# Attention and an ELU feed-forward on one core: where the first two head pairs get their decay sums, and products that nobody reads at the start

## The chip, the cores and the metric

The kernel runs on one core of a Trainium2 chip. Its time is the device time of one execution in microseconds. A core has a matrix engine (TensorE, PE in the profile), a vector engine (VectorE, DVE), a scalar engine (ScalarE, ACT), a general engine (GpSimd, POOL), a queue that issues transfers (SyncE, SP), and 16 DMA engines that carry them.

## The reference, cut to what matters

```python
# q, k, v: 8 batches x 8 heads x 576 rows x 64;  s: 8 x 8 x 576
scores = matmul(q, k.T) / 8
cum    = cumsum(maximum(s, 0))                       # the decay sums, one row per head
bias   = -(cum[..., :, None] - cum[..., None, :])
scores = where(causal, -1e9, scores + minimum(bias, 0))
attn   = softmax(scores)                             # with 1e-9 added to the sum
x      = (attn @ v) as 4608 rows x 512
h      = x @ w_in                                    # 512 x 2048
g      = where(h > 0, h, exp(minimum(h, 0)) - 1)
out    = g @ w_out                                   # 2048 x 512
```

In a causal row the part of the bias that belongs to the query is the same for all keys, and the softmax takes it away. What must be added to the scores is one number per key and head: the head's decay sum.

## The kernel before, in words

Heads are worked in pairs. The first rows (0 to 319, `LOW`) of batches 0 to 2 are done by the class `Low`, twelve units of one pair each; pair 0 and pair 1 of batch 0 are the program's first work. A pair has five score products: one for the first 64 rows of both heads (128 columns) and one per head for two blocks of 128 rows (192 and 320 columns), 1,152 columns together. They are in float32, which TensorE does with two records per product in the trace. VectorE masks each block, scales it and takes the row's minimum (`softmax_block`, line 872), ScalarE takes the exponential with its sum (line 877), VectorE inverts the sums (lines 882 and 883), and any engine scales the block (`normalize`, lines 890 to 894). TensorE then turns the blocks with an identity matrix (lines 680 and 694, tiles `trl`), ScalarE or VectorE copies the turned blocks out of PSUM (lines 381 and 382, tiles `tl`), and TensorE multiplies them with the values (line 675, tile `avl`). After that comes the other attention work and, from 92 us on, the feed-forward (lines 1165 and 1203), which fills most of the time.

The decay sums of a pair ride along in the score product: the tile of keys `kl` has 64 rows of keys, one more row (row 64) with the two heads' sums, and zeros below; the tile of queries `ql` has ones there. Pair 0's sums are worked out alone by `first()` on one partition (lines 430 to 434) and written straight into the row of `kl_first`. All 64 heads' sums are worked out afterwards on 64 partitions in `aux` (lines 445 to 447). Pair 1 gets its row by a transfer from `aux`, every later pair by a transfer from a copy in DRAM, `aux_dram`. Two buffers hold the keys of these units (tag `st`), so pair 2's keys are loaded when pair 0's last score product is done.

Nobody wrote the order by hand. `Plan.issue` keeps a clock for each engine, with a fixed cost for each operation, and always takes the operation that could start first; among those that start together the lower `prio` wins. The order so found is fixed for each engine, and each engine works its list strictly in order. SyncE, too, issues its transfers in that order, and an issue that waits for a buffer holds up all behind it. The weights of the feed-forward come in 512 KB pieces, each with two instructions on VectorE and one on ScalarE to turn it into float32 (lines 531 to 537) and two to split it. Their loads wait for `urgent`, the transfer of pair 1's row.

Blocks of scores may take any of seven PSUM banks (tags `a`, `h`, `o0`, `o1`, `o2`); a turned block may take only the two of tag `a`.

Of the kernel before, what the change touches and what calls it, by code (L numbers as in the profile page):

```python
# [17 lines left out]
P = 128  # L18
# [24 lines left out]
PRIO_LOW = 10  # L43
SP_COST = 430.0

N_FREE = 0


class Buf:
# [18 lines left out]


class Op:  # L70
    __slots__ = ("ways", "after", "before", "behind", "bufs", "new", "prio", "ready", "left")


class Plan:
# [33 lines left out]
    def op(self, prio, ways, reads=(), writes=(), late=()):  # L108

        o = Op()  # L110
        o.ways, o.prio = ways, (prio, len(self.ops))
# [36 lines left out]
        return o  # L148
# [8 lines left out]
    def issue(self):  # L157
# [17 lines left out]
        last = {}  # L175
        n_done = 0
        while pending:
            best = None
            held = slots.get(self.signal, ())
            busy = free["PE"] > DYN_T or held and held[-1].users and not held[-1].others  # L180
            for o in pending:
# [16 lines left out]
                else:  # L198
# [95 lines left out]
def pool_1(n):  # L294
    return 120 + 1.04 * n
# [7 lines left out]
def kernel(  # L303
# [108 lines left out]
        return k, [("Pool-M", pool_1(2 * LOW), lambda: pool.memset(k.v[HB:], 0.0))]  # L412


    k_first, cleared = low_keys("first")

    def decay_sums():

        own = slice(HB, HB + 1)

        def row(m):
            return aux.v.rearrange("p m t -> p (m t)")[own, 2 * m * LOW : 2 * (m + 1) * LOW]

# [13 lines left out]
        def sp():  # L437
            return aux.v[:NB, 0]

        def lo():  # L440
            return aux.v[:NB, 1]

        op(-10, [("DVE-SB", 2700.0, first)], [], [(aux, "row"), (k_first, "sums")])
        for cost, step in (
            (460.0, lambda: dve.tensor_scalar(sp(), sp(), 0.0, None, ALU.max)),
            (1350.0, lambda: dve.tensor_tensor_scan(lo(), sp(), sp(), 0.0, ALU.add, ALU.max)),
            (590.0, lambda: dve.tensor_scalar(
                sp(), lo(), lo()[:, S // 2 : S // 2 + 1], 8.0, ALU.subtract, ALU.mult)),
        ):
            op(-9, [("DVE-SB", cost, step)], [], [(aux, 0), (aux, 1)])  # L450
        load(15, lambda: aux_dram.v[:, 0], sp, [(aux, 0)], [(aux_dram, 0)], NB * S * 4)

    def decay_parts():

        sp, lo, hi = (lambda m=m: aux.v[:NB, m] for m in range(3))
        op(20, [("DVE-SB", 850.0, lambda: dve.tensor_scalar(hi().bitcast(F32R), sp(), 1.0, None, ALU.mult))],
           [(aux, 0)], [(aux, 2)])
        op(20, [("DVE-SB", 750.0, lambda: dve.tensor_tensor(lo().bitcast(F32R), sp(), hi(), ALU.subtract))],
           [(aux, 0), (aux, 2)], [(aux, 1)])
        for m in (2, 1):  # L460
            load(20, lambda m=m: aux_dram.v[:, m], lambda m=m: aux.v[:NB, m], [(aux, m)],
                 [(aux_dram, m)], NB * S * 4)

    def ones():
# [130 lines left out]
    def prepare_low(u):  # L595

        b, j, prio = u.b, u.j, u.prio
        u.vs = vs[u.turn]
        u.k, clear = (k_first, None) if (b, j) == (0, 0) else low_keys(u.tag)
# [5 lines left out]
        op(prio if b or j else -10, [("Pool-M", pool_1(2 * LOW), lambda: pool.memset(u.q.v[HB:], 1.0))],  # L605
           [], [(u.q, "ones")])
        if (b, j) > (0, 0):
            op(prio, clear, [], [(u.k, "sums")])

            src = aux if (b, j) == (0, 1) else aux_dram  # L610
            o = load(prio, lambda: u.k.v[at],
                     lambda: src.v[h0 : h0 + 2, 0, :LOW],
                     [(src, 0)], [(u.k, "sums")], 2 * LOW * 4)
        if (b, j) == (0, 1):
            urgent.append(o)
        n = 1 + 2 * (1 + CUT)

# [7 lines left out]
    def scoring_low(u):  # L625
# [2 lines left out]
        u.first = plan.buf(sb, [P, P], F32, f"pl_{u.tag}", tag=("khs", "vs0")[u.turn])  # L628
        u.pp = {}
        tiles = [(u.first, P)]  # L630

        def pair():
            softmax_block(
                prio, f"{u.tag}_0", True, u.first, P, masks,
                lambda o, w: masks.v.rearrange("p h t -> p (h t)"), [u.k, u.q],
                lambda o, w: ((u.q.v[:, :P], u.k.v[:, :, :HB]),),
                (sm, 0, False, 0, 1.0), view=lambda v: v.rearrange("p (h t) -> p h t", h=2),
            )

        def block(i, h):  # L640
# [8 lines left out]
            if h or u.turn:  # L649
# [2 lines left out]
            softmax_block(  # L652
                prio, f"{u.tag}_{n}", True, pt, pw[i], maskw,
                lambda o, w: maskw.v[:, max(WM - pw[i] + o, 0) :][:, :w], [u.k, u.q],
                lambda o, w: ((u.q.v[:, at], u.k.v[:, h, o : o + w]),),
                (sm, n, n == 2 * CUT, 1 + 2 * CUT, 1.0),
            )
            if n == 2 * CUT:
                for col, (pt, w) in enumerate(tiles):
# [198 lines left out]
    def softmax_block(prio, tag, native, pt, w, mask, mv, reads, operands, inv, view=lambda v: v):  # L858

        n = 1 if w <= 512 else 2  # L860
        mn = plan.buf(sb, [P, 2], F32, f"mn_{tag}", tag="mn", bufs=3)
# [1 line left out]
        for i in range(n):  # L863
            sc = score_bank(f"sc_{tag}_{i}")

            def scores(i=i, sc=sc):
                pairs = operands(i * cw, cw)
                for n, (l, r) in enumerate(pairs):
                    pe_.matmul(view(sc.v[:, :cw]), l, r, start=n == 0, stop=n == len(pairs) - 1)  # L869

            op(prio, [("PE", pe4(cw) if native else 2 * pe(cw), scores)], reads, [sc])
            op(prio, [("DVE", 84 + dve_p(cw), lambda i=i, sc=sc: dve.tensor_tensor_reduce(  # L872
                pt.v[:, i * cw : (i + 1) * cw], sc.v[:, :cw], mv(i * cw, cw), scale,
                BIG if i == 0 else mn.v[:, 0:1], ALU.add, ALU.min, mn.v[:, i : i + 1]))],
               [sc, mask], [(pt, "data"), mn])
# [212 lines left out]
    def attention():  # L1088
# [20 lines left out]
        for u, prepared, scored, weighed in todo:  # L1109
# [5 lines left out]
                behind = []  # L1115
            was = type(u)
            now = scored(u)
            if u is todo[1][0]:
                decay_parts()
            for n in range(max(len(now), len(behind))):  # L1120
                for step in (now[n : n + 1] + behind[n : n + 1]):
                    step()
            behind = weighed(u)
        for step in behind:
            step()
# [120 lines left out]
                t += n  # L1246
        return following

    decay_sums()
    zeros()  # L1250
    mask_tiles()
    for i in range(NQ):
# [93 lines left out]
```

## Time and profile before

| | us |
|---|---|
| median of three runs | 1131.26 |
| lowest and highest | 1130.28, 1135.73 |
| profiled execution | 1133.43 |
| its span in the trace | 1131.7 |
| PE busy | 1096.9 (97%) |
| DVE busy | 843.3 (75%) |
| ACT busy | 628.1 (55%) |
| POOL busy | 451.1 (40%) |

The span is what the trace covers; the execution's own time is 1.7 us longer. The busy time of an engine is the sum of its instructions; what PE lacks to the span, 34.8 us, is the time in which it stood still. A granted clock of 1.00 is 2.4 GHz and 0.50 is 1.2 GHz; a product at 0.50 counts as busy all the same, so the busy share doesn't show the clock.

### The profile page before, as it was taken

Reading aid. Unit: us, or ns where it says so; the run is one execution under the profiler, and the core shown is the slowest. Engines: PE = TensorE matmul, PEld = TensorE weight load, DVE = VectorE, ACT = ScalarE, POOL = GpSimd, SP = SyncE. Lnnn points to the kernel's source line nnn. Section 1 sums busy time; section 2 is a strip of 40 time slices with the busy share of each in tenths; the row PEclk is TensorE's granted clock in tenths of the full one; section 3 lists DMA queues with packets and bytes.
Section 4 is the critical chain, followed back from the end, with each engine's and each line's share of the span. In section 5 each row is a group of like instructions: output and inputs, shape, how many; then the busy total and the mean of one; then the engine's idle time right before and its main releaser. Section 6 shows DMA issues by size and latency. Waiting matters only on the chain.

```text
span 1131.7 us, 19748 instructions
## 1 busy us (share of the span) xinstructions
PE 1096.9 (97%) x5992; PEld 951.6 (84%) x5992; DVE 843.3 (75%) x2133; ACT 628.1 (55%) x1525; POOL 451.1 (40%) x657
## 2 busy tenths in 40 slices
PE   6888999999999999999999999999999999999998
PEld 5677877888788888788888888888888888999997
DVE  6888999778887877687977787878888888432322
ACT  4786766456555655555555555655655556433433
POOL 6664475336444433344434434525544433100000
PEclk8899999999999999999999999999999999999999
DMA  6887688756756855765555666567787686210000
GB/s 173 225 213 201 172 189 193 157 113 152 161 125 128 186 130 121 180 127 133 149 133 118 175 140 136 122 143 172 160 200 155 138 189 151 56 56 1 28 1 28
DMA packets 341689, 156.52 MB, mean 138 GB/s; under 512 B 266424, under 2 KB 320464, under 8 KB 341584
## 3 DMA queue, kind: packets, MB, share of 16 engines
q1 hardware_dynamic: 341584, 155.27, 59.6%
q8 instruction: 48, 0.79, 0.3%
q14 instruction: 57, 0.47, 0.1%
HBM read 79.66 MB, written 19.32 MB: 87 GB/s over the span
## 4 chain that ended last, share of the span: by engine, by line
PE 63%; DVE 6%; DMA 2%; issue 1%; ACT 1%; POOL 1%; SPq 0%; POOLq 0%; DVEq 0%; ACTq 0%
PE o L1203 26%; PE h L1165 25%; PE av L1000 7%; PE sc L869 5%; DVE p L930 2%; DMA stq<-in_qT_dram 1%; DMA T<-p 1%; DVE p L872 1%; DVE h L1187 1%; DVE xl L374 1%; DVE qs L374 0%; DVE x_None L1084 0%; DVE gl L1190 0%; DVE vs L374 0%; DVE g L1182 0%
## 5 line engine op out<-in xcount | busy, mean ns | idle before, releaser
L1165 PE MATMUL h<-xh,wi 128*128 128x384 f32 x1536 | 445.5, 340 | 1.4 <-DVE gl L1190 1.3
L1203 PE MATMUL o<-wo,gh 128*128 128x512 f32 x1152 | 362.5, 396 | 0.1
L1165 PEld LDWEIGHTS h<-xh,wi 128*128 128x128 f32 x1536 | 283.0, 188 | 9.9 <-DVE gl L1190 3.0
L1165 PE MATMUL h<-xl,wi 128*128 128x384 f32 x768 | 258.8, 337 | 0.0
L1203 PEld LDWEIGHTS o<-wo,gh 128*128 128x128 f32 x1152 | 207.3, 188 | 27.4 <-DVE mn L872 0.5
L1203 PE MATMUL o<-wo,gl 128*128 128x512 f32 x576 | 227.8, 395 | 1.0 <-DVE gl L1190 0.8
L1187 DVE SCALAR_TENSOR_TENSOR h<-h,g 128x384 f32<-128x384 f32 x192 | 107.9, 562 | 122.2 <-ACT g L1178 120.6
L1173 ACT ACTIVATE g<-h 128x384 f32<-128x384 f32 x192 | 94.1, 490 | 177.5 <-PE h L1165 167.4
L877 ACT ACTIVATE p<-p,mn 128x192 f32<-128x192 f32 (+1 forms) x232 | 144.9, 625 | 75.1 <-DVE mn L872 72.0
L930 DVE SCALAR_TENSOR_TENSOR p<-p,sm,p 128x512 f16<-128x512 f32 (+3 forms) x239 | 170.7, 742 | 7.6 <-POOL p L922 4.5
L1165 PEld LDWEIGHTS h<-xl,wi 128*128 128x128 f32 x768 | 144.6, 188 | 6.7
L922 POOL TENSOR_SCALAR p<-p,sm 128x512 f16<-128x512 f32 (+3 forms) x125 | 86.9, 702 | 134.3 <-DVE sm L883 53.1
L381 ACT CAST gh<-h 128x384 fp32r<-128x384 f32 x175 | 83.5, 477 | 87.8 <-DVE h L1187 86.6
L1190 DVE TENSOR_TENSOR gl<-h,gh 128x384 fp32r<-128x384 f32 x192 | 106.0, 552 | 32.9 <-ACT gh L381 31.7
L1203 PEld LDWEIGHTS o<-wo,gl 128*128 128x128 f32 x576 | 108.2, 188 | 25.8 <-DVE gl L1190 2.3
L872 DVE CUSTOM_DVE_ANT_0 p<-sc,maskw 128x192 f32<-128x192 f32 (+1 forms) x232 | 109.8, 483 | 25.8 <-PE sc L869 21.4
L1000 PE MATMUL av<-T,vs 128*128 128x256 f16 (+5 forms) x896 | 119.2, 285 | 2.9 <-DMA T<-p 2.1
L1000 PEld LDWEIGHTS <-vs 128*128 128x128 bf16 x896 | 79.7, 98 | 49.8 <-issue 14.3
L375 POOL TENSOR_TENSOR vs<-vs 128x320 f32<-128x320 f32 x72 | 61.0, 848 | 124.6 <-DMA vs<-in_vb_dram 72.1
L869 PE MATMUL sc<-kh,qs 128*128 128x192 f32 (+2 forms) x272 | 87.5, 326 | 2.9 <-DVE mn L872 2.5
L869 PE MATMUL sc<-k,q 128*128 128x192 f32 (+2 forms) x272 | 83.9, 312 | 2.2 <-DMA q<-qs 1.3
L1178 ACT ACTIVATE g<-g 128x384 f32<-128x384 f32 x138 | 72.5, 525 | 4.2
(145 smaller groups left out, 1365.3 us busy)
## 6 DMA issues: line engine op xcount, KB each, us to landing
stk<-in_kT_dram SPq DMA_DIRECT2D x64, 288.0 KB
vs<-in_vb_dram SPq DMA_DIRECT2D x64, 160.0 KB
stq<-in_qT_dram SPq DMA_DIRECT2D x40, 256.0 KB
w_i<-in_w_in_dram SPq DMA_DIRECT2D x16, 512.0 KB
w_o<-in_w_out_dram SPq DMA_DIRECT2D x16, 512.0 KB
out_dram<-ost SPq DMA_DIRECT2D x32, 256.0 KB
x_dram<-x_None SPq DMA_DIRECT2D x20, 288.0 KB
q<-qs SPq DMA_DIRECT2D x40, 128.0 KB
```

Of the source, the lines that this page charges most:

```text
L381: ("ACT", act_c(n), lambda: act.copy(dst(), src())),
L869: pe_.matmul(view(sc.v[:, :cw]), l, r, start=n == 0, stop=n == len(pairs) - 1)
L872: op(prio, [("DVE", 84 + dve_p(cw), lambda i=i, sc=sc: dve.tensor_tensor_reduce(pt.v[:, i * cw : (i + 1) * cw], sc.v[:, :cw], mv(i * cw, c ...
L877: op(prio, [("ACT", 480 + w / 1.2, lambda: act.activation(pt.v[:, :w], pt.v[:, :w], AF.Exp, bias=mn.v[:, n - 1 : n], scale=-1.0, accum_out ...
L922: ("Pool", 160 + 1.04 * n, lambda part=part: pool.tensor_scalar(part(t16, 0), own(part), sm.v[:, r], 1.0, ALU.mult, ALU.mult)),
L930: ("DVE-SB", dve_2(n), lambda part=part: dve.scalar_tensor_tensor(part(t16, 1), own(part), sm.v[:, r], part(t16, 0), ALU.mult, ALU.subtract)),
L1000: op(prio, [("PE", cost, lambda m=m, operands=operands, rows=rows: pe_.matmul(av.v[:rows, dst], *operands(), start=first and m == 0, stop= ...
L1165: pe_.matmul(hp.v[:, :TC], w_in_f[f].v[:, part, c * P : (c + 1) * P], xx.v[:, c, :TC], start=(c == 0 and m == 0), stop=(c == NCB - 1 and m ...
L1173: op(side, [("ACT", act_c(TC), lambda: act.activation(g.v[:, :TC], hp.v[:, :TC], AF.Exp))], [hp], [g])
L1187: op(side, [("DVE", dve_p(TC), lambda: dve.scalar_tensor_tensor(hp.v[:, :TC], hp.v[:, :TC], 0.0, g.v[:, :TC], ALU.max, join[0]))], [g], [hp])
L1190: op(side, [("DVE", dve_p(TC), lambda: dve.tensor_tensor(gl.v[:, :TC], hp.v[:, :TC], gh.v[:, :TC].bitcast(F32), ALU.subtract))], [hp, gh], ...
L1203: pe_.matmul(acc[i].v, g.v[:, tb], w_out_f[f].v[:, part], start=(f == 0 and m == 0), stop=(f == NF - 1 and m == 2),)
```

## The change

Pairs 0 and 1 no longer have a row of sums in their keys. After each score product a second product is added into the same PSUM bank: its stationary operand is `pick`, a 128 x 128 tile with ones in one row (copied from the identity), its moving operand is the first 128 rows of `aux`, of which `pick` selects the head's. This is `picked_sums`, line 651. So `first()` goes, and with it pair 1's transfer. The sums on 64 partitions are worked out in two parts: the first 320 columns at once, the others later (`high()`), after the last masking of the second unit. `aux_dram` gets the first 320 columns alone.

The second part adds transposes of the identity into a PSUM tile that nothing reads, `scratch`. Up to 300 are offered to the planner with the lowest priority and a start that counts as later than it is by `GAP`; those left when the planner's own clock passes `FILL_T` are thrown away. In the order that results there are 31: the first, 28 in a row behind it, and two more. The loads of the first two blocks of weights no longer wait for `urgent` (`N_FREE`), and `urgent` is now pair 2's row.

```diff
-N_FREE = 0
+N_FREE = 2
+FILL_T, GAP = 22e3, 350.0
+N_FILL = 300
+N_PICK = 2
...
+            if free["PE"] > FILL_T:
+                for o in [o for o in pending if o.filler]:
+                    pending.remove(o)
...
-                    rank = (start, o.prio)
+                    rank = (start + GAP if o.filler else start, o.prio)
...
+    picks = [plan.buf(sb, [P, 2, P], F32, f"pick_{j}", tag="gh", bufs=2) for j in range(N_PICK)]
...
-        def first():
-            dve.tensor_scalar(row(0), row(0), 0.0, None, ALU.max)
-            for h in range(2):
-                sp, lo = (row(m)[:, h * LOW : (h + 1) * LOW] for m in range(2))
-                dve.tensor_tensor_scan(lo, sp, sp, 0.0, ALU.add, ALU.max)
-                dve.tensor_scalar(k_first.v[own, h], lo, lo[:, S // 2 : S // 2 + 1], 8.0,
-                                  ALU.subtract, ALU.mult)
...
+        def low():
+            dve.tensor_scalar(sp(first), sp(first), 0.0, None, ALU.max)
+            summed(first)
...
+        for j, t in enumerate(picks):
+            op(-10, [("Pool", 400.0, lambda j=j, t=t: pool.tensor_copy(
+                t.v, ident[:, 2 * j : 2 * j + 2].unsqueeze(2).to_broadcast([P, 2, P])))], [], [t])
...
+        def picked_sums(sc, parts):
+            def step():
+                for n, (h, to, keys) in enumerate(parts):
+                    pe_.matmul(sc.v[:, to], u.pick.v[:, h], aux.v[:, 0, keys],
+                               start=False, stop=n == len(parts) - 1)
...
+    def fillers():
+
+        scratch = plan.buf(ps, [P, DM], F32, "scratch", tag="o2")
+        op(-20, [("PE", 111.0, lambda: pe_.transpose(scratch.v[:, :P], ident, ident))], [], [scratch])
+        for n in range(N_FILL):
+            o = op(1e6 + n, [("PE", 160.0, lambda: pe_.transpose(scratch.v[:, :P], ident, ident))], [(scratch, None)], [])
+            o.filler = True
```

Since the planner deals out all operations by time, the order of all engines differs from there to the end. Three places matter here. The first is PE's first instructions (`sc_0_` and `sc_1_` are the score blocks of pairs 0 and 1). Before:

```order
L869 MATMUL sc_0_0_0_121<-kl_first,ql_0_85 128x128
L869 MATMUL sc_0_1_0_128<-kl_first,ql_0_85 128x192
L869 MATMUL sc_0_2_0_133<-kl_first,ql_0_85 128x192
L869 MATMUL sc_0_3_0_144<-kl_first,ql_0_85 128x320
L869 MATMUL sc_0_4_0_150<-kl_first,ql_0_85 128x320
L869 MATMUL sc_1_0_0_181<-kl_1_89,ql_1_99 128x128
```

And now:

```order
L1281 MATMUL scratch<-ident 128x128
L1283 MATMUL scratch<-ident 128x128 x28
L895 MATMUL sc_0_0_0_156<-kl_0_78,ql_0_85 128x128
L651 MATMUL sc_0_0_0_156<-aux,pick_76 128x64 x2
L895 MATMUL sc_0_1_0_165<-kl_0_78,ql_0_85 128x192
L651 MATMUL sc_0_1_0_165<-aux,pick_76 128x192
```

Twenty-nine transposes stand ahead of pair 0, and each score product has a second one behind it, for pairs 0 and 1. The second place is PE at the scores of pairs 2 and 3 (`trl_1_1` is a turned block of pair 1). Before, after pair 2's fourth block:

```order
L694 MATMUL trl_1_0_307<-ident,p_81 128x128
L694 MATMUL trl_1_0_307<-ident,p_112 128x128
L694 MATMUL trl_1_0_307<-ident,pl_0_1_110 128x128
L694 MATMUL trl_1_0_307<-ident,pl_0_1_135 128x128
L675 MATMUL avl_1_314<-tl_1_303,vs_92 128x128
L694 MATMUL trl_1_1_320<-ident,p_81 128x128
```

And now:

```order
L720 MATMUL trl_1_0_360<-ident,pl_0_1_183 128x128
L895 MATMUL sc_3_0_0_370<-kl_3_267,ql_3_277 128x128
L895 MATMUL sc_3_1_0_376<-kl_3_267,ql_3_277 128x192
L895 MATMUL sc_3_2_0_383<-kl_3_267,ql_3_277 128x192
L895 MATMUL sc_3_3_0_390<-kl_3_267,ql_3_277 128x320
L895 MATMUL sc_3_4_0_394<-kl_3_267,ql_3_277 128x320
L720 MATMUL trl_1_1_427<-ident,p_94 128x128
```

All of pair 3's scores have moved ahead of pair 1's second turned block, and pair 1's products with the values (`avl_1`) behind it. The third place is ACT, where the copy of pair 1's first turned block into `tl_1` stands. Before:

```order
L531 ACTIVATE w_o_201<-w_o_201 128x512
L381 COPY tl_1_303<-trl_1_290 128x128
L877 ACTIVATE pl_2_286,sml_2_305<-pl_2_286,mn_2_0_287 128x128
L877 ACTIVATE p_76,sml_2_305<-p_76,mn_2_1_296 128x192
L877 ACTIVATE pl_0_2_240,sml_2_305<-pl_0_2_240,mn_2_2_312 128x192
```

And now:

```order
L905 ACTIVATE pl_2_342,sml_2_352<-pl_2_342,mn_2_0_343 128x128
L905 ACTIVATE p_89,sml_2_352<-p_89,mn_2_1_350 128x192
L905 ACTIVATE pl_0_2_289,sml_2_352<-pl_0_2_289,mn_2_2_368 128x192
L905 ACTIVATE p_91,sml_2_352<-p_91,mn_2_3_373 128x320
L905 ACTIVATE pl_0_2_297,sml_2_352<-pl_0_2_297,mn_2_4_381 128x320
L905 ACTIVATE pl_3_387,sml_3_397<-pl_3_387,mn_3_0_388 128x128
L549 ACTIVATE w_i_328<-w_i_328 128x512
L922 ACTIVATE p_89<-p_89,sml_2_352 128x192
L922 ACTIVATE pl_0_2_297<-pl_0_2_297,sml_2_352 128x320
L401 COPY tl_1_422<-trl_1_354 128x128
```

The copy stood ahead of pair 2's exponentials and stands behind all five of them now, behind one of pair 3's, a piece of weights and two scalings of pair 2.

## Rows read from the trace of the kernel before

**Rows 1.** The profile's page: span, and busy time by engine.

```profile
span 1131.7 us, 19748 instructions
PE 1096.9 (97%) x5992; PEld 951.6 (84%) x5992; DVE 843.3 (75%) x2133; ACT 628.1 (55%) x1525; POOL 451.1 (40%) x657
```

**Rows 2.** Table by stretch: length, PE, PEld, DVE, ACT, POOL busy, PE's clock, DMA, GB/s.

```profile
0.00:6.47 6.47, 0.00 (x0) 0.03 (x1) 3.32 (x6) 1.28 (x1) 5.50 (x24) 1.00 0.44 112
6.47:10.42 3.95, 3.95 (x10) 2.85 (x10) 3.42 (x10) 1.05 (x5) 3.71 (x11) 1.00 0.76 137
10.42:14.19 3.77, 0.01 (x2) 0.03 (x1) 3.21 (x10) 2.19 (x7) 2.16 (x5) 0.90 0.43 114
14.19:20.30 6.11, 6.11 (x21) 5.23 (x22) 1.53 (x8) 2.30 (x8) 0.41 (x2) 0.50 0.95 270
20.30:30.54 10.24, 8.43 (x52) 7.08 (x50) 8.45 (x28) 8.44 (x26) 7.97 (x15) 1.00 0.70 201
30.54:37.36 6.82, 6.13 (x22) 5.30 (x22) 3.55 (x13) 3.86 (x14) 3.69 (x6) 0.50 0.91 255
37.36:60.00 22.64, 19.78 (x111) 14.95 (x110) 20.93 (x70) 18.64 (x61) 14.39 (x31) 1.00 0.84 219
60.00:92.36 32.36, 29.54 (x181) 24.81 (x180) 28.40 (x94) 27.43 (x90) 20.16 (x43) 1.00 0.77 199
92.36:1131.70 1039.34, 1022.98 (x5604) 891.33 (x5602) 770.50 (x1899) 562.87 (x1319) 393.06 (x524) 1.00 0.59 133
```

**Rows 3.** Timeline of PE: start, length, line, out<-in, shape, count [idle before].

```profile
6.47 3.95 PE L869 MATMUL sc<-kl_first,ql 128*128 128x128 f32 x10 [6.47 <-DVE kl_first L434]
14.19 2.04 PE L869 MATMUL sc<-kl,ql 128*128 128x128 f32 x6 [3.77 <-POOL p L890]
...
17.30 0.63 PE L694 MATMUL trl<-ident,p 128*128 128x128 f32 x2
17.73 0.63 PE L694 MATMUL trl<-ident,pl 128*128 128x128 f32 x2
...
22.53 0.77 PE L869 MATMUL sc<-kl,ql 128*128 128x128 f32 x4
...
25.22 0.38 PE L694 MATMUL trl<-ident,p 128*128 128x128 f32 x2
25.44 0.38 PE L694 MATMUL trl<-ident,pl 128*128 128x128 f32 x2
...
29.68 0.66 PE L675 MATMUL avl<-tl,vs 128*128 128x64 f32 x4 [1.59 <-DVE tl L382]
...
64.30 2.12 PE L869 MATMUL sc<-kl,ql 128*128 128x320 f32 x10
```

**Rows 4.** Timeline of SP: start and length of an issue, its transfer.

```profile
10.50 0.62 SPq L351 DMA_DIRECT2D kl<-in_kT_dram  x1
...
11.87 0.66 SPq L351 DMA_DIRECT2D kl<-aux  x1
```

**Rows 5.** Timeline of DVE at the start: the sums on one partition.

```profile
2.93 0.67 DVE L430 TENSOR_SCALAR aux<-aux 1x640 f32<-1x640 f32 x1 [2.93 <-DMA aux<-in_s_dram]
3.63 0.82 DVE L433 TENSOR_TENSOR_SCAN aux<-aux 1x320 f32<-1x320 f32 x1
4.56 0.53 DVE L434 TENSOR_SCALAR kl_first<-aux 1x320 f32<-1x320 f32 x1
```

**Rows 6.** Timeline of POOL at the start: the identity, and a clearing.

```profile
1.71 0.29 POOL masks.py:199 TENSOR_SCALAR_AFFINE_SELECT ident<-ident 128x128 f32<-128x128 f32 x1
...
2.63 0.63 POOL L605 MEMSET ql<- 64x640 f32 x1
```

**Rows 7.** ACT by line and shape, 0 to 60 us: count, busy us, mean ns.

```profile
L877 ACT ACTIVATE pl<-pl,mn 128x320 f32<-128x320 f32 x7 | 3.9, 560 | 1.8 <-DVE mn L872 1.7
L531 ACT ACTIVATE w_i<-w_i 128x512 f32<-128x512 f32 x5 | 3.3, 663 | 0.0
```

**Rows 8.** Table by stretch, PE alone: 150 to 300 us.

```profile
150.00:300.00 150.00, 144.46 (x783) 1.00 0.74 163
```

More of the change, by code (lines that the diff above doesn't have):

```diff
@@ L44 @@
 SP_COST = 430.0
-N_FREE = 0
+N_FREE = 2
+FILL_T, GAP = 22e3, 350.0
+N_FILL = 300
+N_PICK = 2
+PRIO_HIGH = 12
+PRIO_PARTS = 15
+LATER = 1
 class Buf:
@@ L70 @@
 class Op:
-    __slots__ = ("ways", "after", "before", "behind", "bufs", "new", "prio", "ready", "left")
+    __slots__ = ("ways", "after", "before", "behind", "bufs", "new", "prio", "ready", "left", "filler")
 class Plan:
@@ L177, in issue @@
         while pending:
+            if free["PE"] > FILL_T:
+                for o in [o for o in pending if o.filler]:
+                    pending.remove(o)
+                    for b in o.bufs:
+                        b.users -= 1
+                if not pending:
+                    break
             best = None
@@ L212, in issue @@
             (start, _), o, n = best
+            if o.filler:
+                start -= GAP
             engine, cost, trace = o.ways[n][:3]
@@ new lines, in sp, with lo, summed @@
+        def sp(at=slice(0, S)):
+            return aux.v[:NB, 0, at]
+        def lo(at=slice(0, S)):
+            return aux.v[:NB, 1, at]
+        first, others = slice(0, LOW), slice(LOW, S)
+        def summed(at):
+            dve.tensor_tensor_scan(lo(at), sp(at), sp(at), 0.0, ALU.add, ALU.max)
+            dve.tensor_scalar(sp(at), lo(at), lo()[:, S // 2 : S // 2 + 1], 8.0, ALU.subtract, ALU.mult)
+        def low():
+            dve.tensor_scalar(sp(first), sp(first), 0.0, None, ALU.max)
+            summed(first)
@@ new lines, in high @@
+        def high():
+            dve.tensor_scalar(sp(others), sp(others), 0.0, None, ALU.max)
+            dve.tensor_tensor(sp(slice(LOW, LOW + 1)), sp(slice(LOW, LOW + 1)), lo(slice(LOW - 1, LOW)), ALU.add)
+            summed(others)
+        load(-10, lambda: sp(), lambda: s.rearrange("b h t -> (b h) t"), [], [(aux, 0), (aux, "high")], NB * S * 4)
+        op(-10, [("Pool-M", 350.0, lambda: pool.memset(aux.v[NB:, 0, first], 0.0))], [], [(aux, "below")])
+        op(-10, [("DVE-SB", 1500.0, low)], [], [(aux, 0), (aux, 1)])
@@ L453, in decay_parts @@
+        for j, t in enumerate(picks):
+            op(-10, [("Pool", 400.0, lambda j=j, t=t: pool.tensor_copy(
+                t.v, ident[:, 2 * j : 2 * j + 2].unsqueeze(2).to_broadcast([P, 2, P])))], [], [t])
+        load(-5, lambda: aux_dram.v[:, 0, :LOW], lambda: sp(first), [(aux, 0)], [(aux_dram, 0)], NB * LOW * 4)
+        return lambda late: op(PRIO_HIGH, [("DVE-SB", 1300.0, high)], [], [(aux, "high"), (aux, 1)], late)
     def decay_parts():
         sp, lo, hi = (lambda m=m: aux.v[:NB, m] for m in range(3))
-        op(20, [("DVE-SB", 850.0, lambda: dve.tensor_scalar(hi().bitcast(F32R), sp(), 1.0, None, ALU.mult))],
-           [(aux, 0)], [(aux, 2)])
@@ L460, in decay_parts @@
         for m in (2, 1):
-            load(20, lambda m=m: aux_dram.v[:, m], lambda m=m: aux.v[:NB, m], [(aux, m)],
+            load(PRIO_PARTS, lambda m=m: aux_dram.v[:, m], lambda m=m: aux.v[:NB, m], [(aux, m)],
                  [(aux_dram, m)], NB * S * 4)
@@ L598, in prepare_low @@
         u.vs = vs[u.turn]
-        u.k, clear = (k_first, None) if (b, j) == (0, 0) else low_keys(u.tag)
+        u.pick = picks[j] if b == 0 and j < N_PICK else None
+        u.k, clear = low_keys(u.tag)
         u.q = plan.buf(sb, [P, 2 * LOW], F32, f"ql_{u.tag}", tag="qs", bufs=2)
@@ L604, in prepare_low @@
         load(prio, lambda: u.q.v[:HB], lambda: qT[b, j, :HB, : 2 * LOW], [], [(u.q, "q")], P * LOW * 4)
[L605 to L614, printed above, removed]
+        op(prio, [("Pool-M", pool_1(2 * LOW), lambda: pool.memset(u.q.v[HB:], 1.0))], [], [(u.q, "ones")])
+        op(prio, clear, [], [(u.k, "sums")])
+        if u.pick is None:
+            o = load(prio, lambda: u.k.v[at], lambda: aux_dram.v[h0 : h0 + 2, 0, :LOW], [(aux_dram, 0)],
+                     [(u.k, "sums")], 2 * LOW * 4)
+        if (b, j) == (0, N_PICK):
             urgent.append(o)
@@ L630, in scoring_low @@
         tiles = [(u.first, P)]
+        rows = slice(0, P)
+        def picked_sums(sc, parts):
[3 more added lines that the diff above has]
+                               start=False, stop=n == len(parts) - 1)
+            op(prio, [("PE", sum(pe4(t.stop - t.start) for _, t, _ in parts), step)], [u.pick, (aux, 0), (aux, "below")], [sc])
         def pair():
@@ L635, in pair @@
                 lambda o, w: masks.v.rearrange("p h t -> p (h t)"), [u.k, u.q],
-                lambda o, w: ((u.q.v[:, :P], u.k.v[:, :, :HB]),),
+                lambda o, w: ((u.q.v[rows, :P], u.k.v[rows, :, :HB]),),
                 (sm, 0, False, 0, 1.0), view=lambda v: v.rearrange("p (h t) -> p h t", h=2),
+                picked=u.pick and (picked_sums, [(h, slice(h * HB, (h + 1) * HB), slice(0, HB)) for h in range(2)]),
             )
@@ L654, in block @@
                 lambda o, w: maskw.v[:, max(WM - pw[i] + o, 0) :][:, :w], [u.k, u.q],
-                lambda o, w: ((u.q.v[:, at], u.k.v[:, h, o : o + w]),),
+                lambda o, w: ((u.q.v[rows, at], u.k.v[rows, h, o : o + w]),),
                 (sm, n, n == 2 * CUT, 1 + 2 * CUT, 1.0),
+                picked=u.pick and (picked_sums, [(h, slice(0, pw[i]), slice(0, pw[i]))]),
             )
@@ L868, in scores @@
                 for n, (l, r) in enumerate(pairs):
-                    pe_.matmul(view(sc.v[:, :cw]), l, r, start=n == 0, stop=n == len(pairs) - 1)
+                    pe_.matmul(view(sc.v[:, :cw]), l, r, start=n == 0, stop=n == len(pairs) - 1 and not picked)
             op(prio, [("PE", pe4(cw) if native else 2 * pe(cw), scores)], reads, [sc])
-            op(prio, [("DVE", 84 + dve_p(cw), lambda i=i, sc=sc: dve.tensor_tensor_reduce(
+            if picked:
+                picked[0](sc, picked[1])
+            plan.masked = op(prio, [("DVE", 84 + dve_p(cw), lambda i=i, sc=sc: dve.tensor_tensor_reduce(
                 pt.v[:, i * cw : (i + 1) * cw], sc.v[:, :cw], mv(i * cw, cw), scale,
@@ L1122, in attention @@
                     step()
+            if u is todo[LATER][0]:
+                other_sums([plan.masked])
+                decay_parts()
             behind = weighed(u)
@@ L1247, in moe_chunk @@
         return following
-    decay_sums()
+    def fillers():
[4 more added lines that the diff above has]
+            o.filler = True
+    fillers()
+    other_sums = decay_sums()
     zeros()
```

33 lines of the change are left out of this document (6 added, 27 removed).

## The prediction, made before the change ran

> **What bounds the kernel now.** I read the page first: PE is busy 1096.9 of 1131.7 us [rows 1], so over the whole span PE is the bound, and only what gives PE work earlier, takes work from it or lets its work run faster can move the end. A busy share hides the clock, so the table by stretch comes next [rows 2]. From 92.36 us to the end PE lacks 16.4 of 1039.3 us; nothing of the change aims at that part. Ahead of it PE stands still for 18.4 us (92.36 less the 73.9 of the first eight rows), and runs at 1.2 GHz in two stretches that the table marks 0.50, 14.19 to 20.30 and 30.54 to 37.36. There is a third that the table doesn't show: the clock reads 1.00 from 6.47 to 10.42, but the timeline gives pair 0's five products 3.95 us there, and the same set of ten records takes 2.12 us at 64.30 [rows 3]. I take the durations: half speed, 1.2 GHz.
>
> What PE waits for at the start: until 6.47 for pair 0's sums on VectorE, and then 3.77 us, from 10.42 to 14.19, for pair 1's row. The timeline names a scaling on POOL for that second wait, but those products don't read what POOL scaled. SyncE issued pair 1's row only at 11.87, behind the loads of pair 2's keys, at 10.50, and queries, which waited for pair 0's last product [rows 4]. From issue to use that is 2.32 us. While PE stood still the clock fell (mean 0.90 in that row, 0.50 from 14.19 on), and it rose at 20.30, after unbroken work from 14.19. The second fall, at 30.54, follows a stop from 28.1 to 29.7 [rows 3] in a stretch in which PE was busy 8.43 of 10.24 us [rows 2].
>
> **The change part by part, up to pair 2's first product (22.53 before [rows 3]).**
>
> Start. The identity is ready at 2.00 [rows 6], and 29 transposes stand ahead of pair 0. At 1.2 GHz two take 0.43 us (17.30 to 17.73), at 2.4 GHz 0.22 (25.22 to 25.44) [rows 3]; so the 29 end between 5.2 and 8.2 us. Pair 0 also needs its `kl` and `ql` cleared, which now come late in POOL's list; POOL was busy 5.50 of its first 6.47 us with nearly the same list [rows 2], so not before about 6.75. The start lies between 6.75 and 8.2; I take 7.5, with the clock up shortly before. Against 6.47 that is +1.0.
>
> Are the sums there? On one partition the maximum, scan and subtraction took 0.67 (for 640), 0.82 and 0.53 [rows 5]; 320 columns on 64 partitions cost at most 2.0. If `s` lands as it did, at 2.93, they end at 4.9. The load is now that of 64 rows, whose landing no row shows; VectorE used it from 6.41 before, so at worst 8.4, which would hold up the first added product by 0.7. I take 4.9: hidden behind the fillers.
>
> Pair 0. Five products and as many columns again of added ones: twice 2.12 at 2.4 GHz = 4.2 instead of 3.95: +0.25, ending at 11.7. At 1.2 GHz it would be 7.9.
>
> Pair 1. It needs no row, so the 3.77 us go. Late next is pair 0's scaling, on which pair 0's turned blocks wait; VectorE and ScalarE follow PE block by block, which by my count ends it near 15, and I put 0.4 for it. The work that took 14.19 to 22.53 before was 6.11 us at half speed [rows 2] and 2.23 at full: 5.3 us at full clock. With pair 1's added products (2.1) and the 0.4 it is 7.8 instead of 8.34.
>
> Pair 2 then starts at 11.7 + 7.8 = 19.5, if its row of sums is there. That row stands on SP behind the loads of pair 3, which wait for pair 1's last key product at about 15.4: two issues (0.62 for one at 10.50 [rows 4]) and 2.32 to its use make 19.2. Hidden by 0.3, no more. The weights' 2 MB of early loads lie ahead of it, in a time when the DMA engines were 0.43 to 0.76 busy before [rows 2]; I count no cost, and with that cover gone each us of delay is a us.
>
> Sum so far: 22.53 to 19.5, **-3.0 us**.
>
> **From there to the first feed-forward product (92.36).** The order has changed. All of pair 3's scores stand ahead of pair 1's second turned block, which needs one of two PSUM banks, and the copy that frees it stands on ScalarE behind six exponentials (0.56 for 320 columns, less for the narrower), a piece of weights (0.66) [rows 7], two scalings, and before those more of pair 1 and the weights. Added up from pair 1's last exponential at 19.7 the copy ends near 26.6, while PE is through with pair 3's scores at 24.6. So a stop of some 2 us (0 to 4), and about 1 before it for pair 1's scaling; against 1.8 and 0.7 in the two rows from 20.30 to 37.36: **+1.0 us** (-1.5 to +3).
>
> The clock. Before, the stop at 28.1 was followed by 6.13 busy us at 1.2 GHz, 3.07 lost. The new stop is about as long, but has denser work on both sides; I take it that the clock stays: **-3.1 us**, or 0.
>
> Cover gained. From 37.36 to 92.36 PE stands still for 5.7 us, with VectorE busy 49.3 of 55 us and ScalarE 46.1 [rows 2], much of it weights. In the first 20.3 us they were busy 11.5 and 6.8. The change loads two blocks of weights about 8 us earlier and has `first()` (0.67 and twice 1.35 [rows 5]) off VectorE, so this work moves into the gaps. I give it a quarter of the 5.7: **-1.4 us** (0 to -3).
>
> The rest is dealt out anew with the same operations; I take its 16.4 us of stops as they are. Added `pick` copies, two on POOL, lie beside the fillers.
>
> Sum: -3.0 + 1.0 - 3.1 - 1.4 = -6.5. The profiled execution would go from 1133.43 to 1126.9; it lay 2.2 us above the median of the runs, which goes from 1131.26 to **1124.8**.
>
> **Do transposes raise the clock?** In this trace they stand amid what preceded a rise: from 17.30 to 20.30 eight transposes (the records at 17.30 and 17.73 and four more alike) took 1.7 of 3.0 us, and the clock rose at 20.30 [rows 3]. The Trainium skill (TensorE: Matmul & The Clock Gate, Part 4: PE-mode transpose) says against this that the full clock does not engage for transposes, which don't count as PE-busy in the same way. By that rule the fillers would warm nothing and only delay, and the sum would be the third rival's. The trace doesn't show a rise after transposes alone, so it bears against the rule without settling it.
>
> **The rivals.**
>
> 1. *The new stop lets the clock fall again.* For: a stop of 1.6 us before 29.68 did it. Against: PE stood still 2.9 us in the row from 37.36 to 60 at 1.00. Then the 3.1 don't come: 1127.9.
>
> 2. *The new order is better beyond the start.* From 150 to 300 us alone PE lacks 5.5 us [rows 8], for waits on masking and transfers, and an attention that runs ahead would loosen these. With 3.5 of the 16.4 us gone: 1121.3. Against: nothing in the change aims there.
>
> 3. *The fillers don't raise the clock.* All 29 at 1.2 GHz, start at 8.2 (+0.7); I price the rest by the rise that the rows show, 6.1 us at 0.50 from 14.19 to 20.30: as much at half speed loses 3.0. 1128.5. For: the first work, 3.95 us of products, ran at half speed to its end. Against: the eight transposes above.
>
> 4. *Slower: the newly dealt order costs more after 92 us than the start gives.* The planner goes by its own costs, in which a transfer takes a fixed time; between 92 and 1132 its list has PE stopping 16.4 us, on transfers of queries and turned blocks and on maskings that come late. A list with other neighbours can stop more often, above all from 150 to 300, where the DMA engines are 0.74 busy [rows 8]. It decides from 16.4 + 6.5 = 22.9 us on; at 29 the median is 1137.4. Against: PE has long queues there and three quarters of the stops would have to be added.
>
> That the change would not do what it says: only 31 of 300 fillers are in the order, so the pauses after 20 us stay open; the sum counts on no more.
>
> **How the numbers follow.** Forecast 0.42, rival 1 0.26, rival 2 0.18, rival 3 0.08, rival 4 0.06. What can be told from no change here is 0.5%, 5.7 us: faster means below 1125.6, slower above 1136.9. The forecast lies 0.8 below the limit, so 0.26 of its 0.42 are faster; with rival 2 and 0.04 of rival 1 that is 0.48. Same: 0.16 + 0.22 + 0.08 = 0.46. Slower 0.06. The range: rival 2 with the cover term at its end reaches 1118.5; at the top rivals 1 and 3 with the stop's upper bound reach 1131. Rival 4 and the tails, some 0.15, stay out.
>
> **What would show it.** Right: products of pair 0 taking about 4.2 us for ten and twelve records from 7 to 8 us on, at 1.00; no wait of PE between pairs 0 and 1; pair 2's first product at 19 to 20; a stop near 25 to 27 with the clock at 1.00 through it; the first feed-forward product at 85 to 87. Wrong: 320-column records of 0.68 us in pair 0 (rival 3); 0.50 in the stretch from 24 to 36 (rival 1); PE waiting for the row of pair 2's sums after 20; a first feed-forward product at 86 but an end less than 3 us earlier (rival 4), which would say that the start's gain is given back later.

## The result, and the profile after

The changed kernel takes 1136.53 us (median of 18 runs, 1132.35 to 1140.76), the kernel before, run beside it, 1131.36 (18 runs, 1128.23 to 1136.58). The ratio is 1.0040, 95% interval 1.0027 to 1.0053: about 4.5 us slower. Forecast were 1124.8, range 1118.5 to 1131.0: the time lies outside the range, and it moved the other way. Every ratio below is to runs of the kernel before made beside the runs of that experiment.

The profiled execution of after took 1133.27 us, at the low side of its runs; that of before, 1133.43, lay at the high side. So the two pages have nearly the same span [rows 1] and hide the difference between the medians. After's PE is busier, by the added products and transposes:

```profile
span 1131.3 us, 19840 instructions
PE 1102.6 (97%) x6047; PEld 956.9 (85%) x6047; DVE 848.2 (75%) x2133; ACT 623.3 (55%) x1510; POOL 465.3 (41%) x677
```

PE's timeline at the start answers to [rows 3] (start, length, line, out<-in, shape, count, wait before it):

```profile
2.06 5.37 PE L1283 MATMUL scratch<-ident 128*128 128x128 f32 x28
7.26 0.39 PE L895 MATMUL sc<-kl,ql 128*128 128x128 f32 x2
...
11.39 0.38 PE L895 MATMUL sc<-kl,ql 128*128 128x128 f32 x2
...
20.13 1.68 PE L895 MATMUL sc<-kl,ql 128*128 128x128 f32 x8
...
27.09 0.44 PE L720 MATMUL trl<-ident,p 128*128 128x128 f32 x2 [1.46 <-ACT tl L401]
```

The start went as forecast: pair 0 runs from 7.26 at full speed, pair 1 follows at 11.39 with no wait, pair 2 at 20.13 (forecast 19.5). The table by stretch for after (columns as in [rows 2]) has no cold stretch (time at half clock) there; the last two rows here are those in which it lacks most against before:

```profile
14.19:20.30 6.11, 5.51 (x34) 4.63 (x35) 5.15 (x16) 5.60 (x17) 3.64 (x7) 1.00 0.40 109
20.30:30.54 10.24, 8.38 (x46) 6.30 (x46) 9.64 (x33) 8.58 (x29) 7.61 (x13) 1.00 0.82 239
30.54:37.36 6.82, 4.80 (x33) 4.25 (x34) 6.74 (x19) 4.42 (x16) 5.50 (x10) 1.00 0.88 230
150.00:172.00 22.00, 22.00 (x116) 19.76 (x115) 20.45 (x51) 15.77 (x37) 15.18 (x21) 1.00 0.73 183
172.00:205.00 33.00, 28.61 (x149) 22.27 (x148) 27.21 (x69) 17.30 (x44) 16.95 (x22) 0.95 0.82 172
440.00:706.00 266.00, 262.31 (x1432) 225.78 (x1431) 217.36 (x553) 151.99 (x373) 118.22 (x162) 1.00 0.62 143
```

The same three stretches of the kernel before:

```profile
150.00:172.00 22.00, 19.88 (x107) 16.68 (x106) 19.77 (x42) 14.31 (x34) 15.36 (x19) 1.00 0.96 210
172.00:205.00 33.00, 32.81 (x179) 27.64 (x178) 29.63 (x79) 20.82 (x53) 13.54 (x19) 1.00 0.82 184
440.00:706.00 266.00, 265.12 (x1451) 228.94 (x1448) 206.92 (x537) 148.31 (x359) 115.04 (x153) 1.00 0.62 141
```

In the 33 us from 172 after gets 149 records through and before 179; in the 266 us from 440, 1432 and 1451. Part of the first difference is a matter of where the row begins: before stands still for 2.1 us in the 22 us ahead of it, after not at all, and over 150 to 205 us after is 21 records behind, not 30. From 172 us to its end PE stands still for 17.1 us in after and for 12.1 in before. The list of PE's waits over the whole run names a place (us in total, times, longest), first of after, then of before:

```profile
PE h L1194 <- DVE gl L1219: 8.2, 9, 2.5
```

```profile
PE h L1165 <- DVE gl L1190: 1.3, 3, 0.6
```

`h` has two PSUM banks; the next one comes free when `gl` has read the old one. The longest of these waits, on PE's timeline of after:

```profile
183.62 0.44 PE L1194 MATMUL h<-xh,wi 128*128 128x384 f32 x1 [2.45 <-DVE gl L1219]
...
185.35 0.63 PE L1232 MATMUL o<-wo,gl 128*128 128x512 f32 x1
...
187.66 0.40 PE L1232 MATMUL o<-wo,gl 128*128 128x512 f32 x1
```

After the stop the same product takes 0.63 us, and 0.40 again at 187.66: the clock had fallen to 1.2 GHz. VectorE's timeline ahead of it:

```profile
178.92 0.34 DVE L900 CUSTOM_DVE_ANT_0 p<-sc,maskw 128x192 f32<-128x192 f32 x1
...
180.53 0.34 DVE L1211 TENSOR_SCALAR g<-g 128x384 f32<-128x384 f32 x1
180.80 0.50 DVE L900 CUSTOM_DVE_ANT_0 p<-sc,maskw,mn 128x288 f32<-128x288 f32 x1
...
181.24 0.55 DVE L1216 SCALAR_TENSOR_TENSOR h<-h,g 128x384 f32<-128x384 f32 x1
181.82 0.56 DVE L402 CAST gh<-h 128x384 fp32r<-128x384 f32 x1
182.32 0.59 DVE L910 TENSOR_SCALAR sm<-sm 128x4 f32<-128x4 f32 x1
182.95 0.18 DVE L911 RECIPROCAL sm<-sm 128x4 f32<-128x4 f32 x1
183.04 0.53 DVE L1219 TENSOR_TENSOR gl<-h,gh 128x384 fp32r<-128x384 f32 x1
```

Five maskings of a new unit (the first and the last are shown) stand ahead of the product into `h` and `gh`, and two reciprocal steps between `gh` and `gl`. No instruction of the start runs here; whether it is the planner's new order that costs the time, the runs with a fixed order have to show.

### The profile page after: what moved, and what is told of

Its sections match the earlier page's. It is cut to its first block, busy times and chain, and to the rows that moved or that the text cites. A ratio compares the mean times of both kernels' runs of the same rounds, so it can differ in the third digit from the quotient of the medians.

```text
span 1131.3 us, 19840 instructions
## 1 busy us (share of the span) xinstructions
PE 1102.6 (97%) x6047; PEld 956.9 (85%) x6047; DVE 848.2 (75%) x2133; ACT 623.3 (55%) x1510; POOL 465.3 (41%) x677
## 4 chain that ended last, share of the span: by engine, by line
PE 52%; DVE 4%; issue 1%; DMA 1%; ACT 0%; SPq 0%; DVEq 0%; ACTq 0%
PE o L1232 21%; PE h L1194 21%; PE av L1028 6%; PE sc L895 4%; DVE p L958 1%; DVE gl L1219 0%; DMA vs<-in_vb_dram 0%; DVE h L1216 0%; DVE qs L394 0%; DVE x_None L1112 0%; DVE g L1211 0%; DVE p L900 0%; DMA q<-qs 0%; DMA T<-p 0%; DVE p L952 0%
## 5 line engine op out<-in xcount | busy, mean ns | idle before, releaser
L950 POOL TENSOR_SCALAR p<-p,sm 128x512 f16<-128x512 f32 (+3 forms) x119 | 84.4, 715 | 118.7 <-DVE sm L911 54.1
L395 POOL TENSOR_TENSOR vs<-vs 128x320 f32<-128x320 f32 x85 | 71.7, 844 | 141.7 <-DMA vs<-in_vb_dram 70.0
```

Source lines behind the costliest of these rows:

```text
L950: ("Pool", 160 + 1.04 * n, lambda part=part: pool.tensor_scalar(part(t16, 0), own(part), sm.v[:, r], 1.0, ALU.mult, ALU.mult)),
```

## The experiments

**How an order is held.** The planner normally takes the operation that can start first. To hold one order while the operations change, the kernel carries the list of operations and follows it:

```diff
-            for o in pending:
+            want, way = FOLLOW[n_done]
+            n_done += 1
+            for o in [o for o in pending if o.prio[1] == want]:
```

FOLLOW is the order of one kernel up to a time, and behind it what is left in the order of the other. In names, a is the order of after, b of before; the number is the time of the change of order, the seam, in us on the planner's clock.

**ab20, ab90: the changed operations, after's order for 20 or 90 us, then before's.**

> The changed kernel's operations and its order up to 20 on the planner's clock (fillers, picks, pairs 0 and 1), then the order of the kernel before for all that is left, with the same engine for each operation. Theory 'order' (the start is worth about 5 us, the newly dealt order after it costs 10): about 1126 us, that is 4 to 7 below the kernel before. Rival 'no room' (what the start gains can't be kept, since the rest is held by something other than PE's own work): 1131, as before. Rival 'misfit' (an order is only good behind the start for which it was dealt): 1136 or more.

> The same with the changed kernel's order up to 90 on the planner's clock, where its trace stands 7 to 8 us ahead of the kernel before for equal work, and the order of before for the rest. 'Order': about 1124. 'No room': 1131. 'Misfit': 1136 or more.

ab20: 1131.43 us, ratio 1.0014 (0.9999 to 1.0028). ab90: 1129.53, ratio 1.0001 (0.9985 to 1.0017). The slowdown is gone with the later order. But the theory 'order' had 1126 and 1124, and nothing of a gain is left either; by the numbers alone 'no room' is what came. In ab20 the gain is gone by the first feed-forward product, 92.43 us against 92.36 in before, though pair 2 starts at 20.49.

**ba20, ba90: before's operations, its order for 20 or 90 us, then after's.**

> The kernel before with its own start and order up to 20 on the planner's clock, then the changed kernel's order for all that is left. 'Order': the start's gain is missing and the costly order is there: about 1140. 'No room': 1136, as the changed kernel. 'Misfit': 1136 or more, and this run alone can't tell it from the others.

> The kernel before with its own order up to 90 on the planner's clock, then the changed kernel's order. 'Order': about 1140 to 1143. 'No room': 1131 to 1136.

ba20: 1142.21, ratio 1.0098 (1.0070 to 1.0126). ba90: 1137.91, ratio 1.0076 (1.0052 to 1.0100). After's later order makes the unchanged kernel slow too. ba20 says the less of the two, since its seam costs something itself: PE stands still for 6.11 us ahead of 36.25, a stop that neither kernel has. ba90 lies between the figures of 'no room' and of 'order'. The wait for `gl` goes with the later order, as PE's waits of ba90 show:

```profile
PE h L1352 <- DVE gl L1377: 8.5, 7, 2.6
```

**ab165, ab300: as ab90, changed back at some 170 and 305 us of the trace.**

> The changed operations in the changed kernel's order for its first 170 us or so, and from there in the order of before. Theory 'deal' with the loss at 171 to 205 us and 500 to 700 us only: ratio 0.995 to 0.999, faster than both kernels, and no wait of h for gl over 1.1 us. Theory 'no room' (a lead of the start is waited out in any order, as it was in the order that changed back at 90 us): 0.999 to 1.002.

> The same, changed back at some 305 us. Theory 'deal': the wait of 2 to 2.9 us at 175 to 205 us and the half clock behind it are there again, so 3 to 5 us over the order that changes back at 170 us: ratio 1.000 to 1.003; what is left to the changed kernel's 1.004 is what its order loses at 500 to 700 us. Theory 'no room': within 0.001 of the order that changes back at 170 us.

ab165: 1126.20 us, ratio 0.9965 (0.9950 to 0.9980), faster than both kernels (after 1.0040); with it 'no room' falls. ab300: 1134.06, ratio 1.0019 (1.0001 to 1.0037). Between them lies only the order from 170 to 305 us: 0.0054, 6.1 us, where 3 to 5 were expected; the two intervals don't meet. (The profile of ab300 is of its slowest run, 1136.83.) The stretch 172 to 205 us in the tables of ab165 and of ab300, and the stop on PE's timeline of ab300:

```profile
172.00:205.00 33.00, 32.60 (x180) 26.95 (x179) 29.71 (x72) 18.35 (x45) 13.54 (x17) 1.00 0.76 175
```

```profile
172.00:205.00 33.00, 28.75 (x149) 22.11 (x148) 26.58 (x73) 18.05 (x47) 17.05 (x23) 0.95 0.84 178
```

```profile
186.31 0.44 PE L1383 MATMUL h<-xh,wi 128*128 128x384 f32 x1 [2.65 <-DVE gl L1408]
```

In ab165 VectorE has the steps for `h` between the maskings, and its longest wait for `gl` is 0.6 us (line 1405 is the product into h, 1408 `gl`, 1089 a masking):

```profile
180.10 0.36 DVE L1089 CUSTOM_DVE_ANT_0 p<-sc,maskw 128x192 f32<-128x192 f32 x1 [0.36 <-PE sc L1084]
...
180.59 0.55 DVE L1408 TENSOR_TENSOR gl<-h,gh 128x384 fp32r<-128x384 f32 x1
...
181.51 0.56 DVE L1405 SCALAR_TENSOR_TENSOR h<-h,g 128x384 f32<-128x384 f32 x1
181.98 0.48 DVE L1089 CUSTOM_DVE_ANT_0 p<-sc,maskw 128x320 f32<-128x320 f32 x1
```

ab90 seems to lose by its seam: from 70 to 90 us, around its change of order, PE is busy 16.27 us in ab90 and 18.23 in ab165. That is 2 of the 4 us between the two; the rest isn't placed, and it can be a gain of after's order from 90 to 170 us as well as a loss of ab90.

**glup: after's order, with the steps that free h put ahead in six places.** In FOLLOW, at each place (the dots are other work):

```
before: exp(h) ... g ... h = h, g ... gh ... gl
now:    exp(h), g, h = h, g, gh, gl ...
```

> The changed kernel in its own fixed order, but for six places (those at which the next h waited 0.6 to 2.5 us for gl at 121, 184, 274, 370, 540 and 642 us, 7.2 us in all): there the four instructions that free h (g, the product into h, gh, gl) stand directly behind the exponential on their engine, ahead of the maskings and the reciprocals that stood between them. Theory 'deal, at these stops' (the loss is TensorE waiting at h because the newly dealt order puts gl behind other work of VectorE): the six stops shrink to under 2.5 us, the half clock of 184 to 187 us goes with them, ratio 0.997 to 1.001. Theory 'VectorE is full there' (what is put ahead of gl comes late instead, and TensorE stops for a score's masking or a transposed tile): h's stops go, others of like size come within 10 us, ratio 1.003 to 1.005.

1137.76, ratio 1.0059 (1.0038 to 1.0080): no repair. PE's waits for `gl` shrink from 8.2 to 3.2 us, but others come (after had 2.4 us for `mn`, and none of over 0.6 for `T`):

```profile
PE sc L1084 <- DVE mn L1089: 6.5, 7, 1.8
PE h L1383 <- DVE gl L1408: 3.2, 4, 1.7
PE av L1217 <- DMA T<-p: 3.0, 4, 1.9
```

The longest stop was only shortened, from 2.45 us to 1.74, and is still one for `gl`, since three of the five maskings still run ahead of `g` (178.65 to 179.88):

```profile
182.62 0.45 PE L1383 MATMUL h<-xh,wi 128*128 128x384 f32 x1 [1.74 <-DVE gl L1408]
```

Other stops come close by: 1.89 us at 187.38 for turned blocks, and 1.24 at 121.29 for a masking, where after waited 0.60 at 121.32 for `gl`. PE got 150 records into 172 to 205, after 149, though the cold stretch did not come; so the cold stretch alone is not the loss. This is what the theory "VectorE is full there" says: VectorE was busy 4.97 of the 5 us from 175 to 180. The ratio is above its 1.003 to 1.005, with an interval that reaches into them, and the longest stop stayed, so the run speaks for that theory without proving it. That the order puts too much of a new unit there, and not the wrong instruction first, is argued and not shown.

**redeal_b, redeal_a: an unrelated constant of the planner.**

```diff
-    HOP = 150.0
+    HOP = 149.0
```

in the kernel before, and in the changed kernel

```diff
-SP_COST = 430.0
+SP_COST = 431.0
```

> The kernel before with nothing changed but one constant of the planner that no reader would think of (a hop between engines of 149 instead of 150), which deals the instructions in another order from some 50 us on. Theory 'deal' (each order that the greedy planner deals has its own luck in how it fits the real durations, some us either way): ratio anywhere from 0.993 to 1.007, outside 0.998 to 1.002 more likely than not, with new waits of TensorE at other places. Theory 'room' (what the change itself did to buffers and operations makes any later order slower; orders of the kernel before are alike): ratio 0.999 to 1.001.

> The changed kernel with one constant of the planner one part in 430 higher, which deals another order from some 40 us on. Theory 'deal': another draw, ratio anywhere from 0.993 to 1.007, and the 2.5 us wait of h for gl near 183 us gone or moved. Theory 'room': ratio 1.003 to 1.008 again, with h's waits for gl of 6 us or more in all.

redeal_b: 1139.41, ratio 1.0087 (1.0061 to 1.0113), twice what the change did. Its order differs from some 50 us on, and the same stage suffers, PE busy 47.47 of 55 us from 150 to 205 (52.69 in before), with these waits:

```profile
PE h L1165 <- DVE gl L1190: 6.8, 9, 1.6
...
PE sc L869 <- DVE qs L374: 4.1, 1, 4.1
PE sc L869 <- POOL pl L890: 4.0, 1, 4.0
```

redeal_a: 1132.39, ratio 1.0021 (1.0002 to 1.0039). The stop near 183 us is gone, as 'deal' had it, but the waits of `h` for `gl` are 7.1 us in all, as 'room' had it and nearly after's 8.2; so the sum of these waits doesn't set the time. Its interval reaches into that of the change, so that it is better than after isn't shown; that it isn't much worse is. "Room", by which the changed operations themselves cost time later, falls with ab165.

**bfill: before's order, with transposes in PE's first two waits.** 24 ahead of pair 0, 34 between pairs 0 and 1; their places are in FOLLOW:

```diff
+        scratch = plan.buf(ps, [P, DM], F32, "scratch", tag="o2")
+        op(-20, [("PE", 111.0, lambda: pe_.transpose(scratch.v[:, :P], ident, ident))], [], [scratch])
+        for n in range(N_FILL):
+            op(1e6 + n, [("PE", 160.0, lambda: pe_.transpose(scratch.v[:, :P], ident, ident))], [(scratch, None)], [])
```

> The kernel before with every instruction in its old order, and 58 transposes that nobody reads put in on TensorE alone: 24 ahead of pair 0's first product, 34 between pair 0's last product and pair 1's first. Theory 'clock' (what the start lost at half clock is worth some 3 us in a usual execution): ratio 0.997 to 0.998, 1128 to 1129 us, with the granted clock at 1.00 in 10.4 to 37.4 us. Theory 'one bad execution' (the profiled run of before lost its clock twice, most executions do not, or a lead gained at the start waits it out later, since DVE and the DMAs pace the stretch behind): ratio 0.999 to 1.001.

1127.88, ratio 0.9980 (0.9966 to 0.9994): 2.3 us, at the weak end of the theory "clock". Pair 2's first product is at 18.88 and the stretch from 14.19 to 20.30 at 1.00, but a fall came later, 0.89 and 0.91 in the next two rows. Rows of bfill's timeline and table:

```profile
18.88 0.77 PE L1059 MATMUL sc<-kl,ql 128*128 128x128 f32 x4
```

```profile
14.19:20.30 6.11, 6.11 (x41) 5.43 (x40) 4.17 (x21) 5.01 (x17) 3.16 (x8) 1.00 0.98 303
20.30:30.54 10.24, 7.99 (x45) 6.63 (x44) 6.71 (x24) 8.34 (x26) 8.57 (x15) 0.89 0.67 179
30.54:37.36 6.82, 6.38 (x31) 4.87 (x30) 5.83 (x21) 4.03 (x15) 2.94 (x7) 0.91 0.99 295
```

**nofill: ab90's order with one transpose left of all fillers.** The other entries are taken out of FOLLOW.

> The changed operations in the order that measured 1.0001 (the new order for the first 90 us, then the old one), but of the transposes that fill TensorE's waits only one is left. Theory 'clock': a cold stretch comes back at 7 to 15 us, 2 to 4 us longer than with them, ratio 1.002 to 1.004. Theory 'one bad execution': what TensorE loses at half clock in its first 20 us is waited for again by 90 us, ratio 0.999 to 1.002 and the same first feed-forward product within 1 us.

1130.10, ratio 1.0003 (0.9986 to 1.0021), the same as ab90 with them, as 'one bad execution' had it. The table has 1.00 up to 70 us, but the durations show the cold stretch of the theory 'clock': a product of 320 columns is 1.27 us long at 9.66 and 0.70 at 11.47.

```profile
9.66 1.27 PE L1083 MATMUL sc<-kl,ql 128*128 128x320 f32 x2
...
11.47 0.70 PE L1083 MATMUL sc<-kl,ql 128*128 128x320 f32 x2
```

With a single transpose ahead of it pair 0 starts at 5.68. Pair 2 starts at 21.05, in ab90 at 20.21; at the first feed-forward product the two are 0.3 us apart (83.94 and 83.60). So the fillers bring some 0.8 us at pair 2, and nothing that can be measured at the end. As ab90 keeps nothing of the start's gain, the run can't tell what they are worth in an order that keeps it, as ab165's does.

**again: the kernel before, once more.**

> The kernel before, instruction for instruction, for another profile. Theory 'one bad execution': the half clock at 13.5 to 20.3 us and 30.5 to 37.4 us does not come twice at these places; pair 2's first product is 1 to 3 us earlier than 22.53, and the time 1128 to 1132 us. Theory 'clock' as predicted: both cold stretches again, at the same places within 1 us.

1130.91 us in its one run. Half the expectation held: the first cold stretch came again, the second did not.

```profile
14.19:20.30 6.11, 6.03 (x21) 5.22 (x22) 1.53 (x8) 2.22 (x8) 0.41 (x2) 0.51 0.96 297
...
30.54:37.36 6.82, 6.12 (x38) 5.42 (x39) 5.81 (x19) 4.78 (x18) 4.96 (x9) 1.00 0.94 276
```

Four profiles have before's order up to 37 us. From 14.19 to 20.30 the clock reads 0.50 (before), 0.51 (again), 0.73 (ba90), 1.00 (redeal_b); from 30.54 to 37.36 it reads 0.50, 1.00, 1.00, 1.00. The 1.00 of redeal_b in the first of these rows is not to be trusted, by the durations: two transposes are 0.63 us long there at 17.80, as in [rows 3] at half speed, and 0.38 at 19.38.

```profile
17.80 0.63 PE L694 MATMUL trl<-ident,p 128*128 128x128 f32 x2
...
19.38 0.38 PE L694 MATMUL trl<-ident,pl 128*128 128x128 f32 x2
```

So all four executions have the first cold stretch, until some 17.5 us (ba90), 19.2 (redeal_b) and 20 or a little over (again, before); the second cold stretch is in one of the four.

## Why the prediction was wrong

The step that failed is the last term: "The rest is dealt out anew with the same operations; I take its 16.4 us of stops as they are." It was set to 0 and is +8.5 us by ab165: 1.0040 less 0.9965, times 1131, with an interval of some 2.2 us either way. 6.1 of it lie between 170 and 305 us; the other 2.4 (1.0040 less 1.0019) are no more than their interval. The size depends on the order that it is held against: by ab90 it is 4.4, by ab20 2.9. This is rival 4, by mechanism, place ("150 to 300") and price (1137.4 against 1136.53), to which I gave 0.06; that the price fits so well is luck, since it was set by an assumed 29 us of stops. The argument against it, that three quarters of the stops would have to be added, took the stops of one order as the scale. The scale is what another order costs: redeal_b moved the end by 9.8 us with no reason in the kernel.

- *Up to pair 2, -3.0.* Mechanism right, size one too high: six profiles with after's start have pair 2's first product at 19.52 to 20.71 (after 20.13, forecast 19.5), four with before's at 21.35 to 22.53; the means are 2.0 apart. The forecast took its 22.53 from the latest of the four. nofill has 21.05, so by that one profile about half of the 2.0 is the fillers'.
- *Order from 22 to 37 us, +1.0.* Right: a stop of 1.46 us ahead of 27.09, at full speed behind it. PE stood still 3.9 us in the two rows from 20.30 to 37.36, before 2.5: +1.4.
- *The second cold stretch, -3.1.* Over-sized. It was read from one execution and is in one of four. By this count a quarter of it would have been the price, 0.8. again, which lacks it, has a clock of 0.91 from 70 to 90 us, where before has 1.00, and starts the feed-forward no earlier (92.60).
- *Cover, -1.4.* Right in sign: from 37.36 to 90 PE stood still for 3.4 us in after and 5.7 in before, -2.2.
- *Start in all, -6.5.* ab165, which has after's order up to 170 us and before's behind it, gives -4.0 us (-2.3 to -5.7); with the cold stretch at a quarter the sum would have been -4.2. That they agree is not shown to be more than luck: ab20 and ab90 have the same start and keep nothing of it at the end.
- *First feed-forward product "at 85 to 87".* It is at 83.02, but it counts less than it seems: 366 records stand ahead of it (421 by the table, less 24 of `pick` and 31 fillers), in before 391. A milestone can move by order alone.
- *Slips in the working.* By [rows 3] pair 0 ran at half speed and so did what followed at 14.19; that the clock fell while PE stood still between them is not shown, only the record's reading changed. Pair 2's row comes out at 19.0 (15.4 + 1.24 + 2.32), not 19.2. Rival 2 with the cover term at its end gives 1119.7 (1121.3 less 1.6), not 1118.5. None of these decided the miss.
- *Rival 3* falls. Nothing but transposes ran on PE up to 7.26. Of the 28 that began at 2.06 the last ten begin at 5.90 and the last four at 6.83 (rows below): the first 18 took 0.213 us each, half speed, the last four 0.108, full speed. The Trainium skill (TensorE: Matmul & The Clock Gate, Part 4: PE-mode transpose), by which transposes don't bring the full clock, differs from this measurement for these fp32 ones, and the measurement decides. *Rival 1* falls for after, whose transposes from 27.09 on run at full speed; in redeal_a, which has this stop too (1.74 us) and a later one of 1.93 ahead of 32.05, half speed came behind the later one (0.75 in the row from 30.54). *Rival 2* falls by the end.

```profile
5.90 1.53 PE L1283 MATMUL scratch<-ident 128*128 128x128 f32 x10
...
6.83 0.60 PE L1283 MATMUL scratch<-ident 128*128 128x128 f32 x4
```

Left open: which choice of the planner puts the unit's work so densely at 172 to 187 us. glup shows that moving the steps for h as far as it did is not enough; no order with that unit's maskings moved later was tried.

## What to carry to other kernels

Where a greedy planner lays out the whole program, an edit at the start is two changes, the edit and a new order for all that follows; hold the order fixed beyond the edit to measure the first, at more than one seam, since the seam itself moves the time, and price the second by what an unrelated constant does (here +0.9% in one kernel; 1.0021 for 1.0040 in the other, which isn't clear of noise). Three freshly dealt orders (after, redeal_a, redeal_b) all came out slower than before's, by 0.2 to 0.9%, so the edit is best kept with the old order behind it, the seam tried at a few places: at 20, 90, 170 and 305 us it gave 1.0014, 1.0001, 0.9965 and 1.0019. A price read from one execution's clock needs a second profile before it goes into a sum, and the clock's reading has to be held against the durations of like products.

## What the runs showed of the hardware

- fp32 transposes alone raised PE's clock: of after's 28 the first 18 took 0.213 us each, the last four 0.108, with no other product on PE before them.
- The granted clock can read 1.00 over work at half speed: pair 0 in before [rows 3], pair 0 in nofill (1.27 us for a product at 9.66, 0.70 at 11.47), and redeal_b at 17.80 (0.63 us for two transposes, 0.38 at 19.38).
- The clock's falls at the start are not fixed by the program: of four profiles with the same first 37 us one had half speed from 30.54 to 37.36 and three did not; the first cold stretch, which all had, ended between 17.5 and 20.3.
- Like stops had unlike sequels: behind 1.59 us ahead of 29.68 before went on at half speed, behind 1.55 ahead of 29.61 again did not. Behind the 2.45 us ahead of 183.62 in after a product took 0.63 us for 0.40; behind 2.27 ahead of 194.47 in redeal_a the like product took 0.39.
